# Keeping the first batch's FFT mixing on chip: channels on partitions and transposes by matmul instead of two DRAM bounces, with the filters loaded by SyncE

## The chip, the cores and the metric

The kernel runs on one core of one Trainium2 chip. The metric is the device time of one execution in microseconds (us). The kernel before took 970.11 us (median of 3 runs, 969.6 to 970.21). All times inside a run are read from a profile taken on the chip and count from the first instruction of the span. Five engines appear: PE (TensorE, with PEld for its weight loads), ACT (ScalarE), DVE (VectorE), POOL (GpSimd) and SP (SyncE, which here only issues DMAs). The granted clock is the share of its full clock that TensorE was allowed, as the profile records it.

## The reference, cut to what matters

```python
x: (8, 3008, 256)      filt_r, filt_i: (1505, 256)
X = np.fft.rfft(x, axis=1)
y = np.fft.irfft(X * (filt_r + 1j * filt_i), n=3008, axis=1)

x = y.reshape(8 * 3008, 256)
xn = x / sqrt(mean(x * x, -1) + 1e-6) * rms_g
g = xn @ w_gate                  # 256 -> 1536
out = (g * sigmoid(g) * (xn @ w_val)) @ w_out
```

The FFT of length 3008 = 64 x 47 is done by matmuls in two stages. Stage a transforms over the 64 long axis, stage b over the 47 long axis for each of 32 frequencies k2. Then comes an elementwise complex product with the filters, and then both stages in inverse. Between stage a and stage b the data must change its layout, because stage b contracts over another axis; the same holds between the two inverse stages.

## The kernel before

The eight batches are pipelined: while batch b's feed-forward network (FFN) runs on TensorE, the mixing of batch b+1 is slipped in between. The first batch has nothing to hide behind. All that happens before its first gate matmul is a head in which TensorE is mostly idle, and this study is about that head.

In the kernel before, both layout changes go through DRAM. Stage a's result is stored as `z_tmp` and read back; the inverse stage's result is stored as `g_tmp` and read back.

```python
def z_store(b, c):                                   # first bounce, out ...
    ...
            nc.sync.dma_start(z_d[b, :, r0:r0 + XC, :], t[p0:p0 + 32, :, :])

def t2_load(b, c):                                   # ... and back
    nc.sync.dma_start(t, z_d[b, c * KC:(c + 1) * KC, :, :].rearrange("k p d -> p k d"))

def b_unit(b, i):                                    # stage b and the products
    for u in range(2):
        nc.tensor.matmul(ps[:, u, :], wb[:, k, :], st[b]["t2"][k // KC][:, k % KC, :], ...)
    f1, f2 = fr[c][:, r:r + 2, :], fi[c][:, r:r + 2, :]
    ...
    eng.tensor_tensor(out=s1, in0=ps, in1=f1, op=ALU.mult)
    eng.tensor_tensor(out=s2, in0=ps, in1=f2, op=ALU.mult)

def bi_unit(b, i):                                   # inverse of stage b
    ...
    nc.scalar.activation(out=st[b]["t3"][c][:, 2 * r:2 * r + 2, :], in_=ps[0:KR], func=AXT.Copy)

def g_store(b, c): ...                               # second bounce, out
def t4_load(b, c): ...                               # and back, then norm_first()
```

The filters are loaded by GpSimd in four quarters (c = 0 to 3) into partitions 0 to 54. VectorE copies the real part into the upper half of the partitions, ScalarE the negated imaginary part:

```python
def f_load(c):
    for src, dst in ((filt_r, fr), (filt_i, fi)):
        t = dst[c]
        nc.gpsimd.dma_start(t[0:24, :, :].rearrange("p a d -> p (a d)"),      # 24 rows of 8 KB
                            raw(src, c * KC, [[64 * D, 24], [1, KC * D]]))
        for a, e in ((0, 16), (16, 23)):                                      # 16 and 7 rows
            nc.gpsimd.dma_start(t[32 + a:32 + e, lo:KC, :],                   # of 8 pieces of 1 KB,
                                raw(src, 64 * (a + 1) - c * KC - lo,          # in reverse order
                                    [[64 * D, e - a], [-D, KC - lo], [1, D]]))
        ...
def f_dup(c):
    nc.vector.tensor_copy(out=fr[c][HALF:P], in_=fr[c][0:HALF])
    nc.scalar.activation(out=fi[c][HALF:P], in_=fi[c][0:HALF], func=AXT.Copy, scale=-1.0)
```

## Time and profile before

| | before |
|---|---|
| time, us | 970.11 (969.6 to 970.21) |
| span of the profiled execution, us | 966.1 |
| TensorE busy | 884.5 us, 92% of the span |
| first gate matmul (tile pg) | 83.9 us |
| last filter packet ended | 57.2 us |

The page's first two parts, of the kernel before: busy time, share of the span and instructions of each engine; then the busy share in tenths, and the granted TensorE clock in tenths, in 40 equal slices of the span.

```profile
PE 884.5 (92%) x6095; PEld 553.0 (57%) x6095; DVE 668.8 (69%) x1047; ACT 632.9 (66%) x1066; POOL 376.8 (39%) x325
...
PE   3345978999999999999999999999999999999997
...
PEclk9576999999999999999999999999999999999999
```

One slice is 24 us. From the eighth slice on TensorE is at 9 everywhere but in the last. The first four slices show 3, 3, 4 and 5, and in the second to fourth the clock is low as well. So whatever brings the first gate matmul forward should bring the end forward by about as much.

The tile pg in the kernel before (line, engine, operation, shortest/median/longest ns, first and last start within the first 130 us):

```profile
L382 PE MATMUL pg<-xn,wg x50: 376/379/631, 83.9 to 126.8; 128*128 128x512 f16 x50
```

The chain of waits of the kernel before, between 25 and 85 us (start us, us, what the chain was in):

```profile
31.76 8.66 DMA fi<-in_filt_i_dram
...
40.70 5.76 DMA fi<-in_filt_i_dram
...
51.06 7.24 DMA fi<-in_filt_i_dram
...
60.92 4.16 DMA g_tmp<-t
...
70.58 2.27 DMA g_tmp<-t
...
73.05 2.69 DMA t<-g_tmp
```

Two things hold the head: the filters landing (21.7 us of this chain) and the second bounce (9.1 us). The first bounce is in front of that: stage b's first matmul waits for its reload until 29.5 us. Since every layout change here is a DMA, the copies out of PSUM are plain ones. The groups of instructions up to 84 us, by form (line, engine, operation, output and input with shapes, count, then busy us and mean ns of one, then idle time before):

```profile
L260 ACT ACTIVATE t<-psi 96x512 f16<-96x512 f32 x16 | 9.1, 594 | 8.3 <-DMA g_tmp<-t 7.3 <-PE psi L255 0.9
L196 ACT ACTIVATE t<-psa 128x512 f16<-128x512 f32 x12 | 6.2, 611 | 1.8 <-PE psa L194 1.8
```

Read "busy divided by count" for the rate at which such copies follow each other (6.2 us / 12 = 0.52 us), and the mean for one alone; the mean is larger because neighbours overlap a little.

### The profile page before, as it was taken

To read this page: it belongs to the slowest core of one execution; us is meant where nothing else is said; L and a number is where in the kernel's file an instruction comes from. 1 tells how busy PE (TensorE), PEld (TensorE's weight loads), DVE (VectorE), ACT (ScalarE), POOL (GpSimd) and SP (SyncE) were. 2 spreads that over 40 slices of the span, in tenths; PEclk is the share of its full clock that TensorE was granted. 3 is DMA by queue.
4 is the path that set the end of the run, shared out by engine and by line. 5 is a ranking of instruction groups with operands and counts; after the bars stand their busy time and mean duration, and the time that the engine had idled before them with its cause. 6 is when DMAs were issued, how large, how long until landed. Compare 5 with 4: busy or idle time off the path is not lost.

```text
span 966.1 us, 17361 instructions
## 1 busy us (share of the span) xinstructions
PE 884.5 (92%) x6095; PEld 553.0 (57%) x6095; DVE 668.8 (69%) x1047; ACT 632.9 (66%) x1066; POOL 376.8 (39%) x325
## 2 busy tenths in 40 slices
PE   3345978999999999999999999999999999999997
PEld 1223545565655666666666666566666666666654
DVE  6632445577777888687877878787878888555554
ACT  6343667677766776677766776677756776566543
POOL 3474325325451445335542545135522554033200
PEclk9576999999999999999999999999999999999999
DMA  8869674664447444754457524743345333422211
GB/s 196 142 123 175 152 166 111 151 169 90 91 109 173 94 94 97 161 136 92 93 119 162 123 84 90 174 94 75 99 110 118 88 61 66 113 50 59 44 44 42
DMA packets 94839, 106.99 MB, mean 111 GB/s; under 512 B 17112, under 2 KB 69464, under 8 KB 94560
## 3 DMA queue, kind: packets, MB, share of 16 engines
q1 hardware_dynamic: 85104, 87.92, 37.7%
q0 software_dynamic: 9552, 17.77, 12.0%
q8 instruction: 48, 0.79, 0.4%
q14 instruction: 39, 0.32, 0.1%
q10 hardware_dynamic: 96, 0.20, 0.1%
HBM read 70.62 MB, written 49.90 MB: 125 GB/s over the span
## 4 chain that ended last, share of the span: by engine, by line
PE 77%; DMA 8%; issue 5%; POOL 4%; DVE 4%; ACT 2%; SPq 0%; POOLq 0%; DVEq 0%; ACTq 0%
PE po L398 23%; PE pg L382 22%; PE pv L382 21%; PE psi L255 3%; PE psb L215 2%; DMA fi<-in_filt_i_dram 2%; PE psn L286 2%; PE psa L194 2%; DMA rb<-r_tmp 2%; DVE hh L387 1%; POOL s L246 1%; DVE o L404 1%; PE psq L304 1%; DMA wv<-in_moe_w_val_dram 1%; DMA xc<-in_x_dram 1%
## 5 line engine op out<-in xcount | busy, mean ns | idle before, releaser
L387 DVE TENSOR_TENSOR hh<-pv,sg 128x512 f16<-128x512 f32 (+1 forms) x576 | 391.6, 680 | 233.7 <-ACT sg L386 111.1
L386 ACT ACTIVATE sg<-pg 128x512 f16<-128x512 f32 (+1 forms) x576 | 338.9, 588 | 241.9 <-PE pg L382 225.1
L398 PE MATMUL po<-wo,hh 128*128 128x256 f16 x2304 | 348.3, 272 | 1.7
L382 PE MATMUL pg<-xn,wg 128*128 128x512 f16 (+1 forms) x1152 | 338.4, 375 | 0.0
L382 PE MATMUL pv<-xn,wv 128*128 128x512 f16 (+1 forms) x1152 | 338.4, 375 | 0.0
L398 PEld LDWEIGHTS <-hh 128*128 128x128 f16 x2304 | 220.9, 98 | 113.0 <-issue 12.9
L246 POOL TENSOR_TENSOR s<-s,s 128x512 f16<-128x512 f16 x96 | 110.7, 1153 | 358.7 <-DVE s L243 296.8
L382 PEld LDWEIGHTS <-wv 128*128 128x128 f16 x1152 | 112.8, 98 | 131.7 <-issue 1.4
L367 POOL TENSOR_TENSOR xn<-y,rb 128x1024 f16<-128x1024 f32 x46 | 132.2, 2873 | 54.9 <-DMA rb<-r_tmp 44.6
L243 DVE TENSOR_TENSOR s<-psb,fi 64x512 f16<-64x512 f32 x192 | 132.1, 688 | 6.0
L382 PEld LDWEIGHTS <-wg 128*128 128x128 f16 x1152 | 109.2, 98 | 12.6 <-issue 0.6
L260 ACT ACTIVATE t<-psi 96x512 f16<-96x512 f32 x128 | 75.5, 593 | 25.7 <-PE psi L255 14.0
L291 ACT ACTIVATE y<-psn,gsb 128x512 f32<-128x512 f32 x94 | 64.7, 688 | 13.2 <-PE psn L286 5.2
L310 POOL TENSOR_TENSOR rho<-u,mhalf 128x4 f32<-128x4 f32 x48 | 49.1, 1023 | 59.8 <-DVE u L308 59.5
L255 PEld LDWEIGHTS <-wi 128*128 128x128 f16 x320 | 32.3, 102 | 62.3 <-issue 26.1
L223 DVE TENSOR_TENSOR s<-psb,fr 128x512 f16<-128x512 f32 x96 | 65.4, 682 | 1.2 <-PE psb L215 0.7
L196 ACT ACTIVATE t<-psa 128x512 f16<-128x512 f32 x96 | 56.4, 599 | 13.1 <-PE psa L194 7.5
L215 PE MATMUL psb<-t,wb 96*128 96x256 f16 x256 | 51.5, 285 | 8.9 <-DMA t<-z_tmp 8.3
L296 ACT ACTIVATE sq<-psn 128x512 f16<-128x512 f32 x94 | 55.6, 591 | 0.0
L255 PE MATMUL psi<-s,wi 128*128 128x256 f16 x256 | 46.2, 272 | 8.0 <-ACT sq L296 3.9
L194 PE MATMUL psa<-xc,wa 128*128 128x512 f16 x96 | 36.7, 397 | 17.2 <-DMA xc<-in_x_dram 8.8
L286 PEld LDWEIGHTS <-t 128*128 128x128 f16 x376 | 29.2, 99 | 22.1 <-issue 1.2
(60 smaller groups left out, 382.5 us busy)
## 6 DMA issues: line engine op xcount, KB each, us to landing
out_dram<-o SPq DMA_DIRECT2D x88, 256.0 KB, 3.3
z_tmp<-t SPq DMA_DIRECT2D x128, 96.0 KB, 2.2
t<-z_tmp SPq DMA_DIRECT2D x32, 384.0 KB, 5.0
g_tmp<-t SPq DMA_DIRECT2D x64, 192.0 KB, 3.2
t<-g_tmp SPq DMA_DIRECT2D x126, 96.0 KB, 2.6
rb<-r_tmp SPq DMA_DIRECT2D x46, 256.0 KB, 4.2
xc<-in_x_dram POOLq DMA_DIRECT2D x56, 192.0 KB, 5.6
out_dram<-o SPq DMA_DIRECT2D x8, 192.0 KB, 3.1
```

The source lines that it names most:

```text
L215: nc.tensor.matmul(ps[:, u, :], wb[:, k, :], st[b]["t2"][k // KC][:, k % KC, :], start=True, stop=True)
L223: nc.vector.tensor_tensor(out=s1, in0=ps, in1=f1, op=ALU.mult)
L243: nc.vector.tensor_tensor(out=s2[a], in0=ps[e], in1=f2[e], op=ALU.mult)
L246: nc.gpsimd.tensor_tensor(out=s, in0=s1, in1=s2, op=ALU.add)
L255: nc.tensor.matmul(ps[:, u, :], wi[:, 2 * i + u, q, :], ss[q][:, u, :], start=(q == 0), stop=(q == n - 1))
L260: nc.scalar.activation(out=st[b]["t3"][c][:, 2 * r:2 * r + 2, :], in_=ps[0:KR], func=AXT.Copy)
L291: nc.scalar.activation(out=y[:, dh, :], in_=ps, func=AXT.Identity, scale=gsb[:, dh:dh + 1])
L367: nc.gpsimd.tensor_tensor(out=xv, in0=yv, in1=rv.unsqueeze(1).to_broadcast([P, 2, 4, P]), op=ALU.mult)
L382: nc.tensor.matmul(ps[:, 0:w], wt[:, dt_, ts(jt, P)], xn[:, dt_, 0:w], start=(dt_ == 0), stop=(dt_ == 1))
L386: nc.scalar.activation(out=sg[:, 0:w], in_=pg[:, 0:w], func=AXT.Silu)
L387: nc.vector.tensor_tensor(out=hh[:, 0:w], in0=pv[:, 0:w], in1=sg[:, 0:w], op=ALU.mult)
L398: nc.tensor.matmul(po[s4 // 2][:, s4 % 2, :], hh[:, ts(s4, P)], wo[:, jt, :], start=(jt == 0 and s4 % 2 == 0), stop=(jt == JT - 1 and s4 % ...
```

## The change

The intent: for the first batch alone, both bounces are dropped. Stage a is computed with the channels on the partitions (x as the stationary operand), its result `zt` is kept in SBUF and transposed by matmuls with the identity matrix; the inverse stage likewise gives `gt` with channels on partitions, which is transposed the same way. The layout change is now done by the copies out of PSUM, which write with a step. The filters are issued on SyncE, and the real part is loaded twice, into both halves of the partitions, so that no engine must copy it. The inverse table `wi` comes by DMA and not by 31 transposes. Batches 1 to 7 keep their bounces.

```diff
+    def a0_unit(i, eng):
+        ps = hbank("psa").rearrange("p (a e j) -> p a e j", a=2, e=2)
+        for a in range(2):
+            for dh in range(2):
+                nc.tensor.matmul(ps[:, a, dh, :], st[0]["x"][...][:, ..., ds(dh * P, P)], wat, ...)
+        evac(eng, zt[0][:, :, 0:H * P].rearrange("d e (j p) -> d p e j", p=H)[:, 2 * i:2 * i + 2], ps)
+
+    def t0_unit(i, eng):                 # transposes of zt: matmul against ident
+        ...
+    def bi0_unit(i, eng):                # inverse of stage b, channels on partitions
+        ...
+        evac(eng, gt[0].rearrange("d p (er k) -> d k er p", k=K2)[:, 2 * i:2 * i + 2],
+             ps[:, 0:4 * KR].rearrange("d (k er p) -> d k er p", k=2, er=8))
+    def t4_unit(i, eng, ps=None):        # transposes of gt
+        ...
     def f_load(c):
-        for src, dst in ((filt_r, fr), (filt_i, fi)):
-            t = dst[c]
-            nc.gpsimd.dma_start(t[0:24, :, :]...
+        for src, dst, halves in ((filt_r, fr, (0, HALF)), (filt_i, fi, (0,))):
+            for p0 in halves:
+                t = dst[c]
+                nc.sync.dma_start(t[p0:p0 + 24, :, :]...
...
+        for c in range(NC):
+            wb_load(c)
+            f_load(c)
+            wi_load(c)
+        for i in range(12):
+            a0_unit(i, (nc.scalar, nc.vector)[i % 2])
+        for i in range(22):
+            if i < 16:
+                t0_unit(i, nc.vector if i < 2 or i % 4 == 3 else nc.scalar)
+            if i >= 6:
+                bi0_unit(i - 6, nc.scalar)
+            if i % 4 == 1 and i < 16:
+                f_dup(i // 4, nc.vector)
+            ...
```

The output of an `a0_unit` copy runs over j with p fixed, in a tile where p is innermost with 24 entries of 2 bytes: neighbouring elements land 48 bytes apart. The output of a `bi0_unit` copy steps over 256 entries of 2 bytes: 512 bytes.

## The prediction

> **What bounds the kernel now.** In the 40 slices TensorE is 90% busy or more from about 170 us on; that FFN is not touched. The loss is in the head: the timeline has the first gate matmul (pg) at 83.9 us; before 80 us the table of 10 us windows has TensorE busy 1.2 to 6.2 of each 10 us, at a granted clock of 0.5 to 0.8 from 20 us on. The chain of waits names DMAs: the imaginary filter landing (8.7, 5.8 and 7.2 us between 31 and 58), then the g_tmp bounce: stores 4.2 and 2.3 us, reload 2.7 us; last product at 70.0, first t4 usable at 76.0. The first norm takes to 83.9.
>
> **Removed.** The z bounce (first t2 usable at 29.5, though the a-stage's last copy ended near 16), the g bounce (6 us), 31 transposes making wi, the fr duplication (1.2 to 1.8 us each), and filter issues on GpSimd, which waited for earlier ones to land.
>
> **Added.** 160 transposing matmul pairs and 128 small ones in place of 64 (0.10 to 0.12 us a pair, as the wi transposes show), their copies out of PSUM (0.6 us on ScalarE, 0.69 on VectorE), 1 MB of wi and 1.5 MB of second fr copies by DMA.
>
> **The new limit: the filters' DMA stream on SyncE.** It starts after the third x chunk (about 11.5 us), first bytes about 13. Each quarter moves wb 0.2, fr twice and fi once 0.385 each, wi 0.26 MB: 6.4 MB in all. Issue alone (0.45 us each, about 52) would end at 36 us. Transfers are slower: filter packets of 8 KB took 0.32 us alone but 0.6 to 1.1 under load, into partitions 0 to 54. The Trainium skill, "SBUF — State Buffer", section "Door 1: The DMA port swizzle", says partitions 0 to 63 reach half of the 16 ports, which agrees. I estimate 2.3 us for each 0.385 MB part, 8 us a quarter: the last filter lands near 45.5 us (38 to 57).
>
> VectorE work per quarter (products 0.6 us each, fi negation, wi swap, some copies) is 5 to 7.6 us, under the 8 us, so products follow the stream: last product 7.6 us after it, 53. Then inverse product, copy and t4 transposes 3.6 us, first norm 7 us as before, t4 copies and n units 3 us: first gate matmul near 67, 17 us earlier.
>
> **After that.** Eight t4 copies lie on ScalarE in slots 0 to 3 (4.8 us), but before lost 2.7 us there waiting for rho (93.0 to 95.7), behind GpSimd's queued x loads; I count these even. Batch 1's bounce stalls between 108 and 131 us shift and remain.
>
> **Prediction.** 953 us, 1.8% faster; 8 in 10: 944 to 964. Faster by over 2%: 0.38; within 2%: 0.60; slower: 0.02.
>
> **What would show it.** The chain names filter landings (fr or fi) between 15 and 46 us and no z_tmp or g_tmp before the first gate matmul; VectorE idle ended by those DMAs; last fi product at 50 to 56; first pg at 64 to 70; the FFN from 200 us on as before.
>
> **What would make it wrong.** A stream at 250 GB/s or more leaves VectorE as the limit: first gate matmul near 59, 945 us. A stream near 130 GB/s, as under load before: last filter at 57 to 60, almost no gain. Copies with a 48 or 512 byte output step may be slower than 0.6 us; only the last lies on the path. Slots 0 to 5 may lose more to ScalarE.

## The result, and the profile after

| | before | after |
|---|---|---|
| time in these rounds, us (median, 4 runs each) | 969.86 | 970.35 |
| ratio, 95% interval | | 1.0008 (0.9983 to 1.0032) |
| profiled span, us; mean clock | 966.1; 0.971 | 969.0; 0.972 |
| first gate matmul, us | 83.9 | 83.2 |
| last filter packet, us | 57.2 | 56.8 |

The time is the same. The prediction of 953 us, with 944 to 964 as its range, was wrong. Much moved inside the head, and it came out at the same place, which is a coincidence of gains and losses: the first gate matmul of the kernel after starts at 83.2 us, where 67 was predicted (tile pg, same columns as above).

```profile
L448 PE MATMUL pg<-xn,wg x50: 376/379/634, 83.2 to 127.2; 128*128 128x512 f16 x50
```

The chain of waits of the kernel after, between 10 and 85 us:

```profile
13.14 6.11 DMA fr<-in_filt_r_dram
19.27 5.19 DMA gsb<-in_moe_rms_g_dram
24.52 9.15 DMA fi<-in_filt_i_dram
33.69 9.74 DMA fr<-in_filt_r_dram
43.49 8.74 DMA fr<-in_filt_r_dram
52.25 5.08 DMA fi<-in_filt_i_dram
...
62.49 0.68 DVE hh L304
...
64.43 0.65 PE psi L236 x8
65.11 6.97 ACT gt L202 x4
...
73.20 0.70 DVE t L204
...
83.36 0.85 PE pg L448 x2
```

Both bounces are gone from the chain, as predicted. In their place there is one unbroken row of landings on the one queue, from 13 to 57 us (the gain vector `gsb` is in it only because it was issued on the same queue between two quarters), and at 65.1 us a group of four copies to `gt` of 6.97 us on ScalarE. The groups of instructions of the kernel after, up to 84 us, show these copies and their siblings:

```profile
L202 ACT ACTIVATE gt<-psi 128x384 f16<-128x384 f32 x16 | 29.2, 1971 | 5.9 <-PE psi L236 5.8
L202 ACT ACTIVATE zt<-psa 128x512 f16<-128x512 f32 x6 | 14.2, 2790 | 0.0
L204 DVE CAST zt<-psa 128x512 f16<-128x512 f32 x6 | 14.2, 2699 | 0.0
```

Compare L196 before: the same 512 elements a partition, 0.52 us each there (6.2 / 12), 2.37 us here (14.2 / 6). The `gt` copies of 384 elements take 1.83 us each (29.2 / 16). Divided by the elements that is 4.6 ns an element at the step of 48 bytes, on both engines, and 4.8 ns at the step of 512 bytes, on ScalarE.

The 10 us windows of both kernels show what this did to the engines. First the kernel before, then after (window, length, busy us of each engine with instruction counts, clock, DMA share, GB/s):

```profile
core 0: us, PE busy (x) PEld busy (x) DVE busy (x) ACT busy (x) POOL busy (x), PEclk, DMA share, GB/s
10.00:20.00 10.00, 4.82 (x25) 2.19 (x24) 6.83 (x10) 7.34 (x16) 3.04 (x6) 0.98 0.98 225
...
40.00:50.00 10.00, 4.32 (x24) 2.98 (x24) 7.04 (x10) 7.47 (x10) 5.74 (x7) 0.65 0.64 125
```

```profile
10.00:20.00 10.00, 3.56 (x29) 2.62 (x27) 10.00 (x5) 10.00 (x5) 0.00 (x0) 1.00 0.83 159
...
40.00:50.00 10.00, 6.55 (x67) 5.65 (x64) 3.86 (x7) 10.00 (x10) 2.50 (x2) 0.67 0.75 137
```

VectorE and ScalarE are full between 10 and 20 us with ten copies between them, and ScalarE is full again between 40 and 50. At the same time the DMA engines are three quarters busy or more. So two candidates for the lost gain stand side by side, and the chain alone, which follows one of them, can't tell what the other is worth:

- Theory S, the stream: 6.4 MB come over the SyncE queue at 142 GB/s, and all else waits for it.
- Theory C, the copies: stepped writes four times slower than plain ones fill ScalarE, and all else waits for it.
- Theory B, both: each alone takes about as long as the other, so each hides behind the other.

### The profile page after: what moved, and what is told of

The parts are those of the page before. It is cut to its first block, busy times and chain, and to the rows that moved or that the text cites. A ratio compares the mean times of both kernels' runs of the same rounds, so it can differ in the third digit from the quotient of the medians.

```text
span 969.0 us, 17689 instructions
## 1 busy us (share of the span) xinstructions
PE 893.9 (92%) x6276; PEld 567.0 (59%) x6276; DVE 680.9 (70%) x1055; ACT 660.8 (68%) x1068; POOL 358.4 (37%) x295
## 4 chain that ended last, share of the span: by engine, by line
PE 76%; DMA 10%; DVE 4%; ACT 3%; POOL 2%; issue 2%; SPq 1%; DVEq 0%; POOLq 0%; ACTq 0%
PE po L464 23%; PE pg L448 22%; PE pv L448 21%; PE psi L322 3%; DMA fr<-in_filt_r_dram 3%; PE psb L282 2%; PE psn L352 2%; DMA rb<-r_tmp 2%; PE psa L261 2%; DVE hh L453 2%; DMA fi<-in_filt_i_dram 1%; DMA z_tmp<-t 1%; DVE o L470 1%; PE psq L370 1%; POOL s L313 1%
## 5 line engine op out<-in xcount | busy, mean ns | idle before, releaser
L464 PEld LDWEIGHTS <-hh 128*128 128x128 f16 x2304 | 221.2, 98 | 114.0 <-issue 14.1
L327 ACT ACTIVATE t<-psi 96x512 f16<-96x512 f32 x112 | 66.4, 593 | 18.1 <-PE psi L322 13.9
L357 ACT ACTIVATE y<-psn,gsb 128x512 f32<-128x512 f32 x94 | 64.7, 688 | 10.5 <-PE psn L352 2.6
L263 ACT ACTIVATE t<-psa 128x512 f16<-128x512 f32 x84 | 50.2, 597 | 11.3 <-PE psa L261 5.1
L322 PE MATMUL psi<-s,wi 128*128 128x256 f16 x256 | 46.2, 272 | 8.8 <-POOL s L313 4.1
L322 PEld LDWEIGHTS <-wi 128*128 128x128 f16 x256 | 24.9, 98 | 36.9 <-issue 11.6
L352 PE MATMUL psn<-wai,t 128*128 128x128 f16 x376 | 36.9, 221 | 2.8 <-ACT sq L362 1.4
```

The costliest lines, as they stand in the source:

```text
L322: nc.tensor.matmul(ps[:, u, :], wi[q][:, 2 * i + u, :], ss[q][:, u, :], start=(q == 0), stop=(q == n - 1))
L352: nc.tensor.matmul(ps[:, ts(q, P)], st[b]["t4"][n1p // XC][:, n1p % XC, ds(dh * P, P)], wai, start=True, stop=True)
L464: nc.tensor.matmul(po[s4 // 2][:, s4 % 2, :], hh[:, ts(s4, P)], wo[:, jt, :], start=(jt == 0 and s4 % 2 == 0), stop=(jt == JT - 1 and s4 % ...
```

## The experiments

Fourteen kernels ran. Those said to be wrong give a wrong result and serve for time alone. "First gate matmul" and "last filter packet" (its end on the SyncE queue) are of the one profiled execution. Three kernels have the same loads, and there the last packet ended at 56.8 us (after), 53.9 us (plain copies) and 57.8 us (experiment 4), at 142, 152 and 139 GB/s. So a difference of up to 4 us, or of 9% in rate, between two single profiles is not read as an effect.

### 1. Stream and copies, each taken away alone and both together

All four of the first kernels ran in the same rounds (before in these rounds: 969.72 us, 7 runs).

**No filter loads** (wrong: constants in their place).

```diff
-                    nc.vector.memset(t, 0.0)
+                    nc.vector.memset(t, 0.1)
...
             wb_load(c)
-            f_load(c)
             wi_load(c)
```

> All filter loads left out (tables hold the constant 0.1; wrong result on purpose). Stream theory (the DMA stream alone sets when the head ends): the last fi product moves from 65.5 us to about 52 and the first gate matmul from 83.4 to about 69; time about 956. Copy theory (the strided copies out of PSUM, 2.4 us for zt and 1.9 us for gt, set it through ScalarE): the zt stage still ends at 23.6, ScalarE then has 16 gt copies, 10 t copies and 5 v copies, 41 us in all, to about 65, so the first gate matmul moves to 77 at best and the time to 964. Both together limit: like the copy theory here.

**Plain copies** (wrong: `zt` and `gt` are written in PSUM's own order, without a step).

```diff
-        evac(eng, zt[0][:, :, 0:H * P].rearrange("d e (j p) -> d p e j", p=H)[:, 2 * i:2 * i + 2], ps)
+        evac(eng, zt[0][:, :, 0:H * P].rearrange("d e (p j) -> d p e j", p=H)[:, 2 * i:2 * i + 2], ps)
...
-        evac(eng, gt[0].rearrange("d p (er k) -> d k er p", k=K2)[:, 2 * i:2 * i + 2],
-             ps[:, 0:4 * KR].rearrange("d (k er p) -> d k er p", k=2, er=8))
+        evac(eng, gt[0].rearrange("d p c -> d (p c)")[:, 4 * KR * i:4 * KR * (i + 1)], ps[:, 0:4 * KR])
```

> The same zt and gt copies, same sizes, but with contiguous output (wrong result on purpose); filters loaded as before. Both theories: zt copies 0.6 to 0.7 us, gt copies 0.5 us. Copy theory: the head shrinks to the predicted one, first gate matmul near 67, time 953. Stream theory: last filter still lands at 57, last product near 65, and only the tail of four gt copies (7 us) shrinks: first gate matmul 77 to 79, time about 965.

**Both** (both edits).

> Both taken away (wrong result on purpose). If these two are all that holds the head, VectorE with 28 us of work is left: last product 43 to 46, first gate matmul 57 to 60, time about 945. If something else holds it (first norm, weights, batch 1's bounce), the first gate matmul may come early but the time stays above 955.

| | time, us | ratio to before (95%) | first gate matmul, us |
|---|---|---|---|
| after (in its own rounds, against its own before) | 970.35 | 1.0008 (0.9983 to 1.0032) | 83.2 |
| no filter loads | 964.98 | 0.994 (0.9913 to 0.9966) | 75.8 |
| plain copies | 967.44 | 0.9969 (0.9925 to 1.0013), holds 1 | 75.4 |
| both | 945.78 | 0.9757 (0.9719 to 0.9795) | 56.7 |

Removing the stream alone brings the first gate matmul 7.4 us forward, plain copies alone 7.8 us, both together 26.5 us. The sum of the two single effects is 15.2 us, so 11.3 us appear only when both are gone. In time it is similar: against the ratio of the kernel after, the ratios fall by 0.007, 0.004 (not clear of noise) and 0.025. By the 2% mark only the kernel with both gone is faster. This is theory B; neither of the single theories stands. The starts, in the order of the last three rows:

```profile
L448 PE MATMUL pg<-xn,wg x56: 376/379/634, 75.8 to 129.2; 128*128 128x512 f16 x56
```

```profile
L448 PE MATMUL pg<-xn,wg x56: 376/379/634, 75.4 to 129.3; 128*128 128x512 f16 x56
```

```profile
L448 PE MATMUL pg<-xn,wg x70: 376/379/634, 56.7 to 127.8; 128*128 128x512 f16 x70
```

The chain of the kernel without filter loads shows how the copies alone fill the head:

```profile
9.42 14.12 ACT zt L202 x6
...
54.46 10.27 ACT gt L202 x6
64.77 1.05 PE pst L247 x8
...
76.01 0.85 PE pg L448 x2
```

With no filter to wait for at all, the last `gt` copy ends at 64.7 us, and from there to the first gate matmul the same 11 us pass as in the kernel after (72.1 to 83.4). In the kernel after the stream ends at 56.8 us and the copies' path, freed late by it, still has four of these copies to do.

With both gone, VectorE is the limit, as these two windows of that kernel show (9.83 of 10 us busy):

```profile
20.00:30.00 10.00, 7.40 (x76) 6.34 (x76) 9.83 (x15) 5.73 (x11) 4.21 (x5) 0.68 0.01 2
30.00:40.00 10.00, 5.50 (x69) 4.83 (x70) 9.83 (x12) 4.26 (x9) 3.89 (x3) 0.84 0.01 2
```

### 2. Less stream, with the copies out of the way

The real filter is loaded once, and VectorE copies it to the upper half; plain copies (wrong, same rounds).

```diff
-        for src, dst, halves in ((filt_r, fr, (0, HALF)), (filt_i, fi, (0,))):
+        for src, dst, halves in ((filt_r, fr, (0,)), (filt_i, fi, (0,))):
...
     def f_dup(c, eng):
+            nc.vector.tensor_copy(out=fr[c][HALF:P], in_=fr[c][0:HALF])
```

> Contiguous copies (wrong result) and the real filter loaded once, its upper half copied by VectorE (1.2 us a quarter) in place of the second DMA: 4.9 MB in the stream in place of 6.4. Stream theory, if bytes count: last filter lands near 46, last product 55, first gate matmul 68, time 954. If the second fr copy was free because it lies on the other half of the partitions: last filter still at 55 to 57 and the result is that of the run with contiguous copies alone.

It took 961.24 us, ratio 0.9902 (0.9871 to 0.9933); the last filter packet ended at 46.2 us in place of 53.9 with plain copies, and the first gate matmul started at 69.2 us in place of 75.4. The stream carries 4.87 MB where it carried 6.44, at 141 GB/s, and lasts 34.4 us in place of 42.3. The two intervals overlap, but each of the four runs (960.57 to 961.77 us) is faster than each of the four with plain copies (963.57 to 971.57 us). Once the copies are plain, the bytes matter; the second load of the real filter, which the change introduced to spare VectorE 1.2 us a quarter, costs more than it spares.

### 3. Why the stream is slow

The rate was the term that the prediction had to estimate. I saw three possible reasons: the number of rows of a load, the size of its pieces, and the partitions it reaches. Each has a kernel (s1, s2, s3), and s4 and s5 ask about the rows again; all are on top of the plain copies and all wrong (they load other rows of the filters, with a total size within about 2% of the real one). One run each.

```diff
     # s1: three loads of 16 rows of 8 KB
-                nc.sync.dma_start(t[p0:p0 + 24, :, :]...                 # 24 rows of 8 KB
-                ...
-                    nc.sync.dma_start(t[p0 + 32 + a:p0 + 32 + e, ...]... # 16 and 7 rows of 8 x 1 KB
+                for q0 in (p0, p0 + 16, p0 + 32):
+                    nc.sync.dma_start(t[q0:q0 + 16, :, :].rearrange("p a d -> p (a d)"),
+                                      raw(src, c * KC, [[64 * D, 16], [1, KC * D]]))
     # s2: the same in pieces of 1 KB, in reverse order
+                    nc.sync.dma_start(t[q0:q0 + 16, :, :],
+                                      raw(src, 64 + 7 + c * KC, [[64 * D, 16], [-D, KC], [1, D]]))
     # s3: 128 rows of 1 KB, one for each partition; fr twice (halves is (0, 3)), fi once
+                for a in range(3):
+                    nc.sync.dma_start(dst[c][:, a0 + a, :], raw(src, 256 * c + 128 * a, [[D, P], [1, D]]))
     # s4: as s1, with two loads of 24 rows; s5: as s1, with one load of 48 rows
```

> Base is the run with contiguous copies (e2_contig), where the last fi filter landed at 54.8 us. Each part of a filter table (24 rows of 8 KB, then 16 and 7 rows of 8 x 1 KB, to partitions 0 to 54 of a half) is replaced by three loads of 16 rows of 8 KB to partitions 0 to 47 of the same half; 0.393 MB in place of 0.385 a part, same count of loads, wrong result. If the 1 KB pieces cost the rate: last landing 35 to 42. If the uneven spread over DMA engines (16 rows over 16 engines, 24 over 12, 7 over 7) costs it: 35 to 42 as well. If the half of the partitions costs it[...]: 55 or later.

> As the run before, but each of the three loads is 16 rows of 8 x 1 KB in falling order. Pieces of 1 KB guilty: last landing 55 or later while the run with 8 KB rows is early. Uneven engines guilty: 35 to 42, as early as the run with 8 KB rows. Ports guilty: both late, 55 or later.

> Each load goes to all 128 partitions, 1 KB each, 0.393 MB in three loads a part. Ports (the half of the partitions, few partitions at a time) guilty: last landing 32 to 38, set by the issue on SyncE. Pieces of 1 KB guilty: 50 or later. Only uneven engines guilty: early here too, as in both runs before.

> Contiguous copies, wrong result; each filter part is two loads of 24 rows of 8 KB to partitions 0 to 47 of a half, against three of 16 rows in s1_16x8K (same bytes, same partitions, last filter packet 45.1 us, 196 GB/s). Uneven engines guilty (24 rows on 12 engines, 4 rows on each and 4 engines idle): a third slower, last packet 53 to 57, about 150 GB/s. Ports guilty[...]: last packet 38 to 45, 200 GB/s or more.

> One load of 48 rows of 8 KB a part, same partitions 0 to 47, 3 rows on each of 16 engines as in s1_16x8K. Uneven engines guilty: as s1_16x8K, last packet 43 to 46, 190 to 200 GB/s. Ports at a time guilty: faster, last packet 36 to 42, 215 GB/s or more.

| loads | rate of the queue, GB/s | last filter packet, us | first gate matmul, us | time, us (runs) |
|---|---|---|---|---|
| 24, 16 and 7 rows (plain copies) | 152 | 53.9 | 75.4 | 967.44 (4) |
| s1: 16 rows of 8 KB | 195 | 45.1 | 67.3 | 956.7 (1) |
| s2: 16 rows of 8 x 1 KB | 186 | 46.4 | 67.9 | 958.8 (1) |
| s4: 24 rows of 8 KB | 172 | 49.8 | 71.9 | 960.96 (1) |
| s5: 48 rows of 8 KB | 188 | 46.5 | 67.1 | 953.57 (1) |
| s3: 128 partitions of 1 KB | 241 | 38.9 | 59.8 | 948.17 (1) |

(The rate is the bytes of the SyncE queue's packets from the start of its first filter packet to the end of the last, over that time; the expectation of s4 has 196 where this gives 195. The first row is the plain-copies kernel of experiment 1, with its before at 969.72 us. In the rounds of s1 to s3 the kernel before took 969.59 us, in those of s4 and s5 967.12 us, a single run. The single times are not ranked among each other.)

The DMA view, window 15 to 35 us, gives the share of 16 engines' time that the queue's packets took (packets, MB, share). In order: the plain-copies kernel, s4, s1, s5, s3.

```profile
q1 hardware_dynamic: 2304, 3.12, 85.7%
```

```profile
q1 hardware_dynamic: 1350, 3.25, 82.4%
```

```profile
q1 hardware_dynamic: 1636, 3.83, 103.9%
```

```profile
q1 hardware_dynamic: 1393, 3.83, 102.8%
```

```profile
q1 hardware_dynamic: 4880, 4.78, 81.0%
```

- **Rows that don't divide.** The Trainium skill, "DMA: Bandwidth & Descriptors", section "Why a DMA increments its semaphore by 16 and not by 1", says that a DMA uses the largest number of engines, up to 16, that divides its slowest dimension. 24 rows would then use 12, and 7 rows only 7. The traces agree. They hold the landing events of all DMAs: 9314 in the kernels without filter loads. The 36 loads of 16 rows (s1) add 576, which is 16 each; the 12 loads of 48 rows (s5) add 192, also 16 each; the 24 loads of 24 rows (s4) add 312, which is 13 each, one just after the issue and twelve landings. The kernel after adds 483: 13 for each of 15 loads of 24 rows, 16 for each of 12 of 16 rows, 8 for each of 12 of 7 rows. The shares of the engines' time fit: 82.4% with 24 rows, 103.9% and 102.8% with 16 and 48 (the share sums packets that may overlap, so it can pass 100). What the uneven split costs is less sure: 172 GB/s against 195 and 188, from one profile each, where a third slower (about 150) was expected of uneven engines. s1 reads the same rows three times over, which could help it; s5 hardly does, and has 188. s1 also came between its two expected branches: 45.1 us, where 35 to 42 or 55 and later were expected.
- **The size of a piece** shows no effect that one profile each could tell: 186 GB/s with pieces of 1 KB, 195 with 8 KB, at the same split.
- **The partitions reached.** The Trainium skill, "SBUF — State Buffer", section "Door 1: The DMA port swizzle (why [64,N] ≈ [32,N])", says that partitions 0 to 63 reach 8 of the 16 ports. s3 alone writes both halves with each load, and it is the fastest, 241 GB/s; a packet of 1 KB took 51 ns on average there and 99 ns in s2. That agrees, but the comparison is not pure: s3 also reads its rows in rising order and s2 in falling order. And s3 is not full (81.0%), so something else starts to limit it. Its trace points to the issue on SyncE, as the expectation had it: 48 DMAs are issued from 9.7 to 36.6 us, most of them 0.47 us apart, and SyncE waits for landings for only 4.8 us between them, against 23.1 us in the plain-copies kernel. No run tests this.

So the number of rows, and less purely the partitions, can account for the slow stream. The queue's issue rate is not what holds the kernel after: s3 issues 9 loads a quarter, as many (but for the first quarter), and has the highest rate.

### 4. Full-speed copies with the right result

The stepped write need not have single elements as its runs. Here four rows are gathered in one PSUM bank, interleaved by TensorE (it writes with a step of four elements, 16 bytes), so that the copy reads in order and writes runs of 4 elements of 2 bytes. Same rounds as s1 to s3 (before 969.59 us, 7 runs).

```diff
-        evac(eng, zt[0][...].rearrange("d e (j p) -> d p e j", p=H)[:, 2 * i:2 * i + 2], ps)
+        for a in range(4):
+            nc.tensor.matmul(ps.rearrange("p (j a) -> p a j", a=4)[:, a, :], ..., wat, ...)     # x row 4 * g + a
+        evac(eng, zt[0][:, dh, 0:H * P].rearrange("d (j p) -> d j p", p=H)[:, :, 4 * g:4 * g + 4],
+             ps.rearrange("p (j a) -> p j a", a=4))
     # and the same for gt: two units (four k2) a bank, k innermost
```

> Right result. The zt and gt copies now gather 4 rows in a PSUM bank (TensorE writes PSUM at a step of 16 bytes) and write runs of 4 elements, 8 bytes, in place of single elements 48 or 512 bytes apart; filters as in the changed kernel. If a copy pays for each jump and not for each element: zt 0.6 to 1.0 us, gt 0.5 to 0.8 us, and the run equals the one with contiguous copies: first gate matmul 75 to 78, time 963 to 967. If it pays for each element of any stepped pattern: 2.4 and 1.9 us and 970 as before. TensorE's writes at a step may take twice the 0.3 us of a transpose; that lies off the path.

The groups of instructions up to 84 us, of this kernel:

```profile
L202 ACT ACTIVATE gt<-psi 128x384 f16<-128x384 f32 x16 | 7.9, 491 | 17.9 <-PE psi L238 17.9
...
L202 ACT ACTIVATE zt<-psa 128x512 f16<-128x512 f32 x6 | 3.5, 594 | 3.1 <-PE psa L212 3.1
```

The `gt` copies fall from 29.2 us to 7.9 us in all, the same 0.49 us each as the plain ones of experiment 1. The Trainium skill, "SBUF — State Buffer", the note on "cachelines" in section "Door 1: The DMA port swizzle (why [64,N] ≈ [32,N])", says that SBUF has 16-byte lines, that full bandwidth needs at least two hits per line, and that each access crossing to a new line pays. The rates agree: single elements 48 or 512 bytes apart are slow, and runs of four elements cost nothing more than plain copies. Part of the cost moved to TensorE: its `psi` matmuls with a 16-byte step follow each other at 160 ns where the unstepped ones did at 80 ns, both at a granted clock of 0.5, which agrees with the skill's page "PSUM — Partial Sum Buffer", section "Specifications (TRN2)" (8-byte lines, non-contiguous access slows matmuls). Some of that lies on the chain of waits: its last 32 `psi` matmuls take 3.98 us there, and 2.56 us in the plain-copies kernel. This kernel's line first, then the plain one's:

```profile
65.83 3.98 PE psi L238 x32
```

```profile
61.94 2.56 PE psi L236 x32
```

The time, though, is 969.66 us, ratio 1.0002 (0.997 to 1.0034), with the right result, and the first gate matmul starts at 80.8 us:

```profile
L452 PE MATMUL pg<-xn,wg x52: 376/379/634, 80.8 to 129.8; 128*128 128x512 f16 x52
```

Both miss the expectation (963 to 967 us, 75 to 78 us): its last filter packet ended at 57.8 us, 3.9 us after that of the plain-copies kernel, and the slower matmuls come on top. Removing the copies' cost while keeping the stream brings next to nothing, as theory B says. In time it can't be told from the plain-copies kernel, since the intervals overlap.

### 5. Both mended, with the right result

On top of the 8-byte runs, the real filter is loaded once (as in 2.), and in a second kernel the imaginary filter goes to the upper half and the real one to the lower, with the signs turned where they are used, so that neighbouring loads alternate between the halves. Same rounds (before 968.67 us, 11 runs).

```diff
     # one load of fr
-        for src, dst, halves in ((filt_r, fr, (0, HALF)), (filt_i, fi, (0,))):
+        for src, dst, halves in ((filt_r, fr, (0,)), (filt_i, fi, (0,))):
     # fi up, in the second kernel
+        for src, dst, halves in ((filt_r, fr, (0,)), (filt_i, fi, (HALF,))):
+            nc.vector.tensor_copy(out=fr[c][HALF:P], in_=fr[c][0:HALF])
+            nc.vector.tensor_scalar(out=fi[c][0:HALF], in0=fi[c][HALF:P], scalar1=-1.0, ...)
     # not shown: the memsets of the halves, the swapped inverse table negated, and
     # "add" turned into "subtract" where later batches sum the products
```

> Right result. Copies in runs of 8 bytes as in e6_runs8; fr loaded once, into the lower half, upper half copied by VectorE: 4.9 MB in the stream in place of 6.4, all filters to partitions 0 to 54. From the run with one load and contiguous copies (last filter at 46 to 47, first gate matmul 69.2, 961 us): last filter 45 to 48, first gate matmul 69 to 73, time 960 to 964.

> Right result. Same bytes as e8_onefr_runs8, but fi is loaded into the upper half (partitions 64 to 118) and its negative made in the lower half; the sign is turned back in the wi copy and in GpSimd's sum of later batches. If what limits the stream is which half of the partitions the loads go to: last filter at 36 to 41, VectorE (33 us of work from 16 us on) ends the products at 50 to 54, first gate matmul 63 to 67, time 953 to 957. If it is the uneven spread over DMA engines or the bytes as such: last filter 45 to 48 and 960 to 964, as the run before.

| | time, us | ratio to before (95%) | last filter packet, us | rate, GB/s | first gate matmul, us |
|---|---|---|---|---|---|
| one load of fr | 958.58 | 0.9912 (0.9879 to 0.9946) | 48.3 | 135 | 69.4 |
| fi in the upper half | 954.4 | 0.9866 (0.9841 to 0.9892) | 45.4 | 144 | 66.2 |

Both are right in their results. The second is, with the last kernel of this section, the fastest right one, 1.3% under the kernel before, which by the 2% mark still counts as the same. With the halves alternating, the rate was 144 GB/s against 135. The Trainium skill, "SBUF — State Buffer", section "Can I just issue two DMAs to hit both halves?", gives +6% for two DMAs into the two halves; the runs here neither confirm nor refute it, since the kernel of experiment 2, with the loads of the first of these kernels, had 141 GB/s. The expectation came out half and half: the stream as if the halves did not matter (45 to 48 us), the time as if they did (953 to 957 us). The two kernels' intervals overlap, so what the second gained over the first stays open. Its tile pg:

```profile
L452 PE MATMUL pg<-xn,wg x62: 376/379/634, 66.2 to 127.2; 128*128 128x512 f16 x62
```

By 127.2 us it has begun 62 of them, where the kernels before and after had begun 50. VectorE is now nearly full in the middle of the head (9.83 of 10 us from 30 to 40, 9.79 from 40 to 50), so I tried two ways to relieve what seemed next.

**Copies of fr on ScalarE** (same rounds).

```diff
-            nc.vector.tensor_copy(out=fr[c][HALF:P], in_=fr[c][0:HALF])
+            nc.scalar.activation(out=fr[c][HALF:P], in_=fr[c][0:HALF], func=AXT.Copy)
```

> As e7_fiup_runs8, with the fr copies on ScalarE (1.9 us each) in place of VectorE (1.2 us). If VectorE ends the head there: 3 to 5 us earlier, first gate matmul 60 to 64, time 950 to 954, about 1.7 to 2% under the kernel before. If the stream still ends it: no difference.

A miss: 957.55 us, ratio 0.9893 (0.9873 to 0.9912), no gain over the kernel it builds on, and the first gate matmul at 72.3 us. The waits of ScalarE in that kernel (what waited, for what: us in total, times, longest):

```profile
ACT gt L202 <- PE psi L238: 12.4, 10, 5.2
ACT fr L512 <- DMA fr<-in_filt_r_dram: 10.7, 4, 4.3
```

Put in ScalarE's order ahead of other copies, the four copies of fr make it wait 10.7 us for the filters in this trace, and what stands behind them starts later. The work was small; its place in the order is the likely cost (no run moves it elsewhere in the order).

**The 7-row loads on GpSimd's queue** (own rounds, before 970.22 us, 7 runs).

```diff
-                    nc.sync.dma_start(t[p0 + 32 + a:p0 + 32 + e, lo:KC, :],
+                    (nc.gpsimd if a else nc.sync).dma_start(t[p0 + 32 + a:p0 + 32 + e, lo:KC, :],
```

> Right result. As e7_fiup_runs8 (954.4 us; filter packets from 12.0 to 45.1 us), with the loads of 7 rows issued from GpSimd's queue in place of SyncE's: same rows, same bytes. If the rows pile up on the first few DMA engines when SyncE splits 24, 16 and 7 rows, SyncE's share falls from 4 to 3 rows on the fullest engine: last filter packet at 36 to 41, last product 50 to 52, first gate matmul 62 to 65, time 950 to 953. If not: last packet still at 44 to 47 and 953 to 957.

Also a miss: 956.81 us, ratio 0.9863 (0.9843 to 0.9883), no different from the kernel it builds on. SyncE's filter packets ran from 14.1 to 44.1 us and did not end at 36 to 41, at 143 GB/s, about as before: the queue's time fell from 33.4 to 30.0 us, no more than the bytes taken from it, and it started 2.1 us later. The first gate matmul came at 69.0 us, later than the 66.2 us of the kernel it builds on. So although 7-row loads use few engines, moving them to another queue does not raise the rate of the rest. The Trainium skill, "DMA: Bandwidth & Descriptors", section "Issuing engines are not separate DMA queues", would have told me so: all issuers share the same 16 DMA engines, and a second one saves only issue time. The run agrees (143 GB/s, against 144 in the kernel it builds on).

### 6. What is given back after the first gate matmul

The lead at the first gate matmul is not all found at the end. From the table of starts of the FFN's gate activations (tile sg), in the profiled executions, as lead over the kernel before in us (negative is earlier):

| | activation 0 | 12 | 30 | 60 | 100 | end |
|---|---|---|---|---|---|---|
| after | -0.7 | -0.2 | +1.3 | +1.9 | +2.3 | +2.9 |
| both gone (experiment 1) | -27.2 | -26.2 | -25.0 | -22.4 | -21.5 | -21.5 |
| fi in the upper half | -17.7 | -17.1 | -15.5 | -15.5 | -14.4 | -14.7 |

Between activation 12 and activation 100 these kernels lose 2.5, 4.7 and 2.7 us. The kernel after loses 2.5 us too, while it has no lead, so this is not what hid the gain, but it takes a part of any. Up to activation 12 the lead holds to within 1.0 us, as the prediction had said ("I count these even"). One part can be seen in the windows: each of these three kernels has one 10 us window between 100 and 150 us in which the granted clock is 0.83 on average, where the kernel before has 1.00 in all of them. A loss of 0.17 of 10 us is at most 1.7 us. The rest, around the stalls of batch 1's bounces, which the change leaves, is not settled.

## Why the prediction was wrong

The mechanism was named rightly: with the bounces gone, the filters' stream on SyncE is on the chain from 13 to 57 us. Two terms of the sum were mis-sized, and a claim about the second was wrong.

| step, as predicted | predicted | measured |
|---|---|---|
| stream's first bytes | about 13 us | 11.9 us: near |
| "8 us a quarter" | 8 us | 11.2 us (11.9 to 56.8 us, four quarters): wrong |
| "the last filter lands near 45.5 us" | 45.5 (38 to 57) | 56.8 us: at the edge of its range |
| stage a's copies | 0.6 to 0.69 us each | 2.37 us each; the stage ends at 23.6 us |
| last product after the stream | 7.6 us | 8.7 us: right |
| "inverse product, copy and t4 transposes 3.6 us" | 3.6 us | 7.7 us: wrong |
| last fi product | 50 to 56 us | 65.5 us |
| first norm; t4 copies and n units | 7 us; 3 us | 7.1 us (with the first t4 copy); 3.0 us: right |
| first gate matmul | 67 us | 83.2 us |
| lead after that, to activation 12 | even | even; 2.5 to 4.7 us lost later |

1. **The stream's rate was the step that failed first.** "2.3 us for each 0.385 MB part" and so "8 us a quarter" was an estimate from packets under the load of the kernel before. The stream measured 11.2 us a quarter, 3.2 us more. Its last packet ended 11.3 us later than predicted (56.8 against 45.5), of the 16.2 us by which the first gate matmul came late (83.2 against 67). The prediction saw the risk itself: "A stream near 130 GB/s ... almost no gain". It knew that 64 partitions reach half of the ports, but did not count that loads of 24 and 7 rows leave engines idle; with loads of 16 rows throughout the rate was 195 GB/s in place of 152 (one profile each).
2. **"Copies with a 48 or 512 byte output step may be slower than 0.6 us; only the last lies on the path" was wrong.** They were four times slower, and that makes ScalarE as long a path as the stream. Four copies of 6.97 us in all, not one of 0.6, lay between the last product and the transposes, and that step took 7.7 us in place of 3.6. With the last filter at 56.8 us the prediction's own sum would still give 78.3 us for the first gate matmul; most of the 4.9 us from there to 83.2 is this step. The decisive run is the one without filters: with nothing to wait for, the first gate matmul is still at 75.8 us.
3. **Even a right stream would not have saved the prediction.** With the copies as they are, removing the stream wholly gave 964.98 us. The predicted 953 needed both terms to be right; the version with both mended in part reached 954.4 us with its first gate matmul at 66.2 us, near the predicted 67. From its last filter packet (45.4 us) to the first gate matmul it took 20.8 us, where the prediction had 21.5, so the rest of the sum is of the right size. That the times nearly meet is partly luck: this kernel loads fewer bytes at a lower rate, gives VectorE more copies, and against its own before is 1.3% faster, not 1.8%.

## What to carry to other kernels

When a change takes out one wait, cost everything that then runs in parallel with the chain to the same care, because the second path is only hidden and not free; take away the two suspects both singly and together (a two by two), since here each alone gave 0.4% (within the noise) to 0.7% and both 2.5%. A layout change done by a copy's output step was slow with single 2-byte elements and free of that cost with runs of four, so gather elements into runs before copying (runs of two were not tried). Give loads a row count that 16 divides, and before moving work onto another engine look at what would then wait behind it for a DMA.

## What the Trainium skill lacked or had wrong

- "SBUF — State Buffer", the note on cachelines: it has no figure for what a stepped write costs. "Vector Engine (DVE) Microarchitecture Reference" has some for VectorE and 4-byte words; no page that I found has one for ScalarE or for 2-byte elements copied out of PSUM. The runs show 4.6 ns an element at a step of 48 bytes on both engines and 4.8 ns at 512 bytes on ScalarE, against 1.3 ns for the same `gt` copy without a step or in runs of 8 bytes (0.49 us for 384 elements).
- "PSUM — Partial Sum Buffer", "Specifications (TRN2)": "slows matmuls significantly" has no figure. At a step of 16 bytes, matmuls of 96 columns follow each other at 160 ns in place of 80 ns, both at a granted clock of 0.5.
- "DMA: Bandwidth & Descriptors": the rule for the number of engines is there, but not what an uneven split costs: 152 GB/s with 24, 16 and 7 rows, 172 with 24 and 24, 195 with 16, 16 and 16 (one profile each).
- "SBUF — State Buffer" has rates for single transfers into 64 and 128 partitions; no page that I found has the time of a packet in a full queue of loads: 1 KB took 99 ns into one half of the partitions (s2), and 51 ns with all 128 (s3).
